# Eighteen loads of up to 62 KB a row in place of twenty-one of up to 54 KB, with V cut into units

## The chip, the cores and the metric

The kernel runs on one NeuronCore of one Trainium2 chip. Its five engines each follow their own instruction list: TensorE (PE in the profile), VectorE (DVE), ScalarE (ACT), GpSimd (POOL) and SyncE (SP), which here issues all transfers. Data comes from the chip's memory (HBM) over 16 DMA engines into the on-chip memory SBUF, which has 128 rows (partitions); matmul results go to PSUM banks. The metric is the device time of one execution in microseconds (us), as the median of several.

## The reference

One decode step (one new token, batch B = 2) of a block in which attention and a gated layer stand side by side:

```python
xn = layernorm(x)                       # x: (2, 1, 512)
q = (xn @ wq) -> 32 heads of 128
k, v = the last W = 2048 positions of k_cache, v_cache   # (2, 32, 2048, 128) each
p = softmax(q @ k.T * 128**-0.5)
att = (p @ v) -> (2, 1, 4096) @ wo
glu = ((xn @ w_gate) * (xn @ w_up)) @ w_down             # F = 1376
return x + att + glu
```

All is 32-bit floating point. K and V of one head are 2 MB each (2 x 2048 x 128 x 4 bytes), so 32 heads are 134 MB; with the weights 159.5 MB are read once, and little is computed on each number.

## The kernel before

**Layout.** The host writes all data in the order of use into one array, `stream`. A *load* is one transfer of that array: for each of the 128 rows of SBUF one contiguous piece of up to `STEP` = 54 KB. A *field* is a part of a load: K of head h (16 KB a row, written K5 below for head 5) with the part of `wq` that belongs to it (2 KB), V of head h (16 KB) with its rows of `wo` (2 KB), and the weights of the gated layer (`wg`, `wu`, `wd`, `wr`). `blocks` (line 54) returns the list of loads with their fields; host and kernel both use it. Behind a small load `f` come loads 0 to 20 (up to V of head 27), which are of 42 to 54 KB a row, and then the tail: load 21 (K31, V28), two of 18 KB (V29, V30), V31 with 16 KB, and three of 8, 4 and 2 KB. From K3 on, K and V alternate, V by LAG = 3 heads behind its K, three of the two kinds in each load: K V K in one, V K V in the next.

**Slots.** Three slots of 54 KB a row (`step0` to `step2`) take the loads in turn. `pump` (line 280) issues the next load when a slot has come free; `done` (line 301) counts the fields of a load that have been used, and calls `pump` at the last one. All loads go through SP's queue, in order. The instructions of all engines are written down in program order (`Flow.add`), and each waits for those earlier ones whose bytes it needs or overwrites. A load into a used slot therefore waits only for the instructions on the bytes that it overwrites. `x_nat` and `carry`, two transfers of a few KB, are issued behind the first three large loads.

**Work on a head.** For each K: DVE multiplies it by q (`products`, line 416) and sums over the 128 elements (`sums`), in place in the slot; maximum over a row and then over rows by POOL (`maxima`), exponentials by ACT (`weights`), whose result `p` stands in a ring of NP = 6 tiles, and the sum's reciprocal (`reciprocals`). PE projects q for a later group of four heads (`project_q`, line 399). For each V: `weigh` (line 468) multiplies it by p with 8 matmuls on PE, one for each 2 KB of the row (a *unit*); ACT copies the result (`copy_out`), PE transposes it with 4 matmuls (`transpose`), ACT scales it, and PE multiplies it by `wo` into the bank `acc` (`project_o`, line 504). `values` (line 518) does this for one head or for two at once, which share a bank, the copy and the transposes.

**Order.** The main loop (line 592) goes through the loads; behind the first K of a load stand all its V (`values(vs)`). PE works in program order, so a V matmul that waits for its load holds all that stands behind it. Heads 30 and 31 and the tail stand written out from line 617 on: `products(30)`, `sums(30)`, `values([26, 27])` of load 20, then V28, V29, V30, V31 each when its load has come, with some matmuls on other data (`keep_busy`) in between. DVE copies `acc` into SBUF (line 631) between products and sums of head 31.

The record of operations has one line, 226 (in `Flow.emit`), for all instructions; operations are told apart by their tiles: `step` is a slot, `q<-step,xnb` is `project_q`, `o_ps<-step,p` is `weigh`, `tr<-first,o_sb` is `transpose`, `acc<-step,oT` is `project_o`, `q<-xnb,mean_w` is `keep_busy`.

Of the kernel before, what the change touches and what calls it, by code (L numbers as in the profile page):

```python
# [14 lines left out]
P = 128  # L15
B, D, H, DH, SK, F = 2, 512, 32, 128, 8192, 1376
W = min(4096, max(256, SK // 4))
J = W // P
NC = D // P
FB = 4 * P  # L20
# [4 lines left out]
LAG = 3  # L25
# [6 lines left out]
GC = HG * DH  # L32
JG = J // 4
CK, CQ, CO = B * J * DH, NC * GC, D
CP = CQ // NC
UNIT = CK + max(CP, CO)
STEP = 3 * UNIT
WD = [(0, 2), (2, 4), (4, 7), (7, NFC - 1), (NFC - 1, NFC)]
NS = 3
BUFS = 3  # L40
# [13 lines left out]
def blocks():  # L54

    def wd(n):
        return [("wd", i, D) for i in range(*WD[n])]

    def k(h):
        return [("k", h, CK)] + ([("wq", h, CP)] if h + HG < H else [])

    def v(h):
        return [("v", h, CK), ("wo", h, CO)]  # L70

    def gu(half):
        n = NC * (FH[half][1] - FH[half][0])
        return [("wg", half, n), ("wu", half, n)]

    units = []
    for h in range(LAG, H - 1):
        units += [k(h), v(h - LAG)]
    ones = [("pick", 0, 8 * B), ("rows", 0, NFB * B)]
    first = [("x", 0, B * NC)] + ones + [("w", 0, NC * DH)]  # L80
    loads = [[("w", 1, CQ - NC * DH)] + k(0) + k(1), gu(0) + k(2)]
    loads += [gu(1) + units[0] + units[1] + wd(0) + [("wr", 0, NS * P)]]
    loads += [sum(units[i : i + 3], []) for i in range(2, len(units), 3)]
    loads += [k(H - 1) + v(H - 1 - LAG) + wd(1)]
    out = [(("f", 0), first)] + [(("s", i), fields) for i, fields in enumerate(loads)]
    late, last = ("s", len(loads)), ("s", len(loads) + 1)
    out += [(late, v(H - 3)), (late, v(H - 2)), (last, [("v", H - 1, CK)])]
    out += [(last, [("wo", H - 1, CO)] + wd(2))]
    return out + [(last, wd(n)) for n in range(3, len(WD))]


class Flow:
# [15 lines left out]
    def tile(self, shape, name, offset=None):  # L108
        if offset is None:
            size = -(-4 * math.prod(shape[1:]) // 32) * 32  # L110
            if self.low <= BASE < self.low + size:
                self.low = BASE + BUFS * 4 * STEP
            offset, self.low = self.low, self.low + size
# [141 lines left out]
def sliding_attention_plus_glu_kernel(  # L255
# [20 lines left out]
    tiles, used, left, got = {}, {}, {}, {}  # L276
# [54 lines left out]
        dve.memset(t, 0.0)  # L331
    gu_ps = o_ps

    NP = 6
    p_ring = [flow.tile([P, B, JG, 8 * B], f"p{i}") for i in range(NP)]
    for t in p_ring:
        pl.memset(t, 0.0)
# [40 lines left out]
    def side(h):  # L378

        return int(h % 3 == 0)  # L380
# [104 lines left out]
    def transpose(heads, o_sb):  # L485
        d = tr[:, 8 + 4 * bank : 12 + 4 * bank]
        s0, s1 = side(heads[0]), side(heads[-1]) + 1
        dst = d.rearrange("p (s b) -> p s b", b=B)[:, s0:s1, :]
        for r in range(4):
            pe.matmul(  # L490
                dst, o_sb[:, r * DH : (r + 1) * DH], pick[:, r, s0:s1, :],
                start=(r == 0), stop=(r == 3),
            )
        for h in heads:
            rec = rec_t.pop(h)
            oT[h] = oT_ring[h % 4]
            for b in range(B):
                c = B * side(h) + b
                act.activation(
                    oT[h][:, RB * b : RB * b + 1], d[:, c : c + 1], AF.Copy,  # L500
                    scale=rec[:, b : b + 1],
                )

    def project_o(h):
        wo = got["wo", h][0]
        if h < HF:
            pe.matmul(acc, oT.pop(h), wo, start=(h == 0), stop=False)
        else:
            accumulate(oT.pop(h), wo)
        done("wo", h)  # L510

    def pv(heads):
        for h in heads:
            weigh(h, got["v", h][0], range(CK // FB), h == heads[0], h == heads[-1])
            done("v", h)
        return copy_out()

    def values(heads, busy=((), ())):
        o_sb = pv(heads)
        for n in busy[0]:  # L520
            keep_busy(n)
        transpose(heads, o_sb)
        for n in busy[1]:
            keep_busy(n)
        for h in heads:
            project_o(h)


    hT = flow.tile([P, 4, NFB, M], "hT")
    dve.memset(hT, 0.0)  # L530
# [4 lines left out]
    def project_gu(half):  # L535
        lo, hi = FH[half]
        for w, kind in enumerate(("wg", "wu")):
            t = got[kind, half][0].rearrange("p (c f) -> p c f", c=NC)
            for c in range(NC):
                for n in range(2 * half, min(2 * half + 2, NFB)):  # L540
                    f0, f1 = n * FB, min(n * FB + FB, F)
                    pe.matmul(
                        gu_ps[w][32 * n : 32 * n + B, 0 : f1 - f0],
                        xn[:, c, :], t[:, c, f0 - lo : f1 - lo],
                        start=(c == 0), stop=(c == NC - 1),
                    )
            done(kind, half)
# [41 lines left out]
    spare_in = xnb.rearrange("p a b -> p (a b)")  # L589
    for i in range(2):  # L590
        project_first(i)
    for _, fields in blocks():
        ks = [i for kind, i, _ in fields if kind == "k"]
        vs = [i for kind, i, _ in fields if kind == "v"]
        if vs and vs[-1] >= H - 5:
            break
        for n, h in enumerate(ks):
            products(h)
            project_q(h)
            if 2 <= h <= 3:  # L600
                project_gu(h - 2)
            sums(h)
            if h == LAG:
                gate()
            if vs and n == 0:
                values(vs)
            if h == LAG:
                down(0)
                down_rest()
            maxima(h)  # L610
            weights(h)
            if h >= 1:
                reciprocals(h - 1)
# [3 lines left out]
    h = H - 2  # L617
# [1 line left out]
    spare, o_ps2 = spare_t[:, 0, :], spare_t[:, 1, :]  # L619
    products(h)  # L620
    sums(h)
    values([H - 6, H - 5], ((GC, 256), (GC,)))
    keep_busy(GC)
    maxima(h)
    reciprocals(h - 1)
# [1 line left out]
    o_sb = pv([HF])  # L627
# [7 lines left out]
    accumulate(carry, acc_sb)  # L635
    project_o(HF)
    weights(h)
    values([H - 3], ((GC,), (GC,)))
    maxima(h + 1)
    reciprocals(h)  # L640
    weights(h + 1)
# [2 lines left out]
    o_sb = pv([H - 2])  # L644
# [5 lines left out]
    o_sb = flow.ring([P, 4 * DH], "o_sb", 2)  # L650
    v = got["v", H - 1][0].rearrange("p (n k w) -> p n k w", k=2, w=2 * DH)
    for k, t in enumerate((o_ps[bank], o_ps2)):
        for n in range(CK // FB):
            b, i = divmod(n, JG)
# [19 lines left out]
def laid_out(x):  # L674

    import numpy as np

    a = x["A_x"].reshape(B, D)
    first = {
        kind: np.zeros((P, w), a.dtype) for kind, _, w in blocks()[0][1][:3]  # L680
    }
    carry = np.zeros((M, M), a.dtype)
    first["x"][:] = a.reshape(B, P, NC).transpose(1, 0, 2).reshape(P, B * NC)
    for b in range(B):
        for r in range(4):
            for s in range(2):
                first["pick"][8 * s + 4 * b + r :: 32, (2 * r + s) * B + b] = 1.0
        for n in range(NFB):
            first["rows"][32 * n + b, n * B + b] = 1.0
        carry[RB * b, RB * b] = 1.0  # L690
    cache = {
        kind: x[name][:, :, SK - W :, :].reshape(B, H, P, J * DH).transpose(1, 2, 0, 3)
        for kind, name in (("k", "A_k_cache"), ("v", "A_v_cache"))
    }
    wq = x["A_wq"].reshape(P, NC, H // HG, GC).transpose(2, 0, 1, 3)
    wo = x["A_wo"].reshape(H, P, D)
    gu = {
        kind: x[name].reshape(P, NC, F)
        for kind, name in (("wg", "B_w_gate"), ("wu", "B_w_up"))
    }  # L700
    wd = x["B_w_down"]
    rest = wd[NFC * P :].reshape(FR, NS + 1, P)

    def field(kind, i):
        if kind in first:
            return first[kind]
        if kind in ("k", "v"):
            return cache[kind][i].reshape(P, CK)
        if kind == "w":
            return (wq[0][:, :, DH:] if i else wq[0][:, :, :DH]).reshape(P, -1)  # L710
        if kind == "wq":
            return wq[i // HG + 1][:, i % HG, :]
        if kind == "wo":
            return wo[i]
        if kind == "wr":
            last = rest[:, NS, :].reshape(NS, FX, P).swapaxes(0, 1)
            return np.concatenate([rest[:, :NS, :], last]).reshape(P, NS * P)
        if kind == "wd":
            return wd[i * P : (i + 1) * P]
        return gu[kind][:, :, FH[i][0] : FH[i][1]].reshape(P, -1)  # L720

    def part(fields):
        rows = [field(kind, i) for kind, i, _ in fields]
        rows.append(np.zeros((P, pitch(fields) - sum(w for _, _, w in fields)), a.dtype))
        return np.concatenate(rows, axis=1).ravel()

    parts = [part(fields) for _, fields in blocks()]
    x_rows = np.zeros((D // P, 32 // RB, P), a.dtype)
    x_rows[:, :B] = a.reshape(B, D // P, P).transpose(1, 0, 2)
    return {  # L730
        "x_rows": x_rows.reshape(-1, P),
        "carry": carry,
        "stream": np.concatenate(parts),
    }
# [30 lines left out]
```

## Time and profile before

| | |
|---|---|
| median of 3 runs | 375.95 us (375.94 to 376.26) |
| the profiled execution | 376.07 us, its span 374.7 us |
| read from HBM | 159.47 MB |
| packets on the one DMA queue | 4370 |
| mean granted clock of TensorE | 0.80 of full speed |
| instructions | 2767 |

The span runs from the first to the last instruction; 1.4 us lie around it. A row of the timeline gives the start, the length, the engine, the operation with its output and inputs, how many records are merged in the row (`x16`), and in brackets how long the engine stood idle before it and what ended that. A matmul of 32-bit numbers leaves two records. In the rows of DMA issues the last number is the median time from issue to landing.

### The profile page before, as it was taken

How to read it: one execution, taken by the hardware profiler on the slowest of the kernel's cores; microseconds unless marked ns; L12 is line 12 of the kernel's file. 1: busy time of each engine (PE TensorE's matmuls, PEld its weight loads, DVE VectorE, ACT ScalarE, POOL GpSimd, SP SyncE). 2: the span in 40 equal slices, each digit the busy share in tenths (PEclk: the TensorE clock that was granted, in tenths of full speed). 3: DMA queues.
4: the chain of work that ended last, by engine and by line, in shares of the span. 5: the costliest groups of instructions: out<-in, count | busy, mean ns of one | idle time of the engine just before them, and what ended most of it. 6: DMA issues, size and time to landing. Idle time of an engine off the chain costs nothing.

```text
span 374.7 us, 2767 instructions
## 1 busy us (share of the span) xinstructions
PE 254.7 (68%) x1100; PEld 87.9 (23%) x1100; DVE 294.6 (79%) x147; ACT 58.7 (16%) x259; POOL 25.3 (7%) x78
## 2 busy tenths in 40 slices
PE   3386686986548486854848685485867548646997
PEld 3241122331112122211212221122212112121344
DVE  3299691998599499859949986994997699599960
ACT  1021001122020211202121120111202011121132
POOL 1001000000000000000000010000010000000010
PEclk9796988899696966859686688976668887656999
DMA  8999999899999999999999999999999999999996
GB/s 333 460 437 455 403 433 472 378 472 410 438 460 396 460 413 444 449 401 460 407 445 443 419 455 413 443 439 413 461 419 437 439 403 437 446 443 417 414 427 254
DMA packets 4382, 159.70 MB, mean 426 GB/s; under 512 B 514, under 2 KB 658, under 8 KB 1042
## 3 DMA queue, kind: packets, MB, share of 16 engines
q1 hardware_dynamic: 4370, 159.54, 98.7%
q8 instruction: 8, 0.13, 0.1%
q14 instruction: 4, 0.03, 0.0%
HBM read 159.47 MB, written 0.07 MB: 426 GB/s over the span
## 4 chain that ended last, share of the span: by engine, by line
DMA 69%; DVE 17%; PE 12%; ACT 1%; issue 1%; SPq 0%
DMA step<-in_stream_dram 69%; DVE step L226 8%; DVE s L226 8%; PE o_ps L226 4%; PE acc L226 4%; PE q L226 2%; PE tr L226 2%; ACT o_sb L226 0%; ACT oT L226 0%; SPq L226 0%; ACT hT L226 0%; DVE o_sb L226 0%; DVE m L226 0%; ACT hX L226 0%; DVE o_out L226 0%
## 5 line engine op out<-in xcount | busy, mean ns | idle before, releaser
L226 DVE TENSOR_TENSOR step<-step,q 128x4096 f32<-128x4096 f32 x31 | 136.7, 4408 | 53.2 <-DMA step<-in_stream_dram 53.2
L226 PE MATMUL q<-step,xnb 128*128 128x512 f32 (+1 forms) x128 | 92.3, 870 | 77.4 <-DMA step<-in_stream_dram 77.4
L226 DVE TENSOR_REDUCE s<-step 128x32 f32<-128x4096 f32 x32 | 141.4, 4419 | 1.1
L226 PE MATMUL o_ps<-step,p 128*16 128x512 f32 (+1 forms) x512 | 69.1, 677 | 10.5 <-DMA step<-in_stream_dram 10.4
L226 PEld LDWEIGHTS q<-step,xnb 128*128 128x128 f32 x128 | 32.0, 274 | 130.2 <-DMA step<-in_stream_dram 93.7
L226 PE MATMUL acc<-step,oT 128*9 128x512 f32 (+1 forms) x88 | 34.6, 548 | 9.0 <-ACT oT L226 9.0
L226 PE MATMUL tr<-first,o_sb 128*128 128x2 f32 (+2 forms) x198 | 27.7, 258 | 15.4 <-ACT o_sb L226 12.8
L226 ACT COPY o_sb<-o_ps 128x512 f32<-128x512 f32 (+1 forms) x24 | 13.9, 577 | 143.4 <-PE o_ps L226 143.4
L226 PEld LDWEIGHTS tr<-first,o_sb 128*128 128x128 f32 x198 | 25.6, 197 | 37.1 <-ACT o_sb L226 32.3
L226 POOL PARTITION_ALL_REDUCE mm<-m x32 | 11.3, 355 | 285.3 <-DVE m L226 274.8
L226 PEld LDWEIGHTS o_ps<-step,p 128*16 128x16 f32 x512 | 13.5, 106 | 70.6 <-issue 55.0
L226 ACT ACTIVATE nm<-mm 128x2 f32<-128x2 f32 x32 | 6.5, 203 | 129.2 <-POOL mm L226 129.2
L226 ACT ACTIVATE p<-s,nm 128x16 f32<-128x16 f32 x64 | 19.2, 300 | 1.0
L226 ACT ACTIVATE oT<-tr,rec 128x1 f32<-128x1 f32 x64 | 12.2, 260 | 28.3 <-PE tr L226 28.3
L226 POOL PARTITION_ALL_REDUCE sum<-rs x32 | 12.7, 398 | 52.5 <-ACT p L226 52.5
L226 PE MATMUL o_ps<-step,xn 128*2 128x512 f32 (+1 forms) x48 | 12.8, 586 | 0.0
L226 ACT ACTIVATION_READ_ACCUMULATOR p<-s,nm 128x1 f32 x64 | 11.9, 187 | 0.0
L226 DVE TENSOR_TENSOR step<-step,tr 128x4096 f32<-128x4096 f32 x1 | 4.4, 4420 | 9.5 <-DMA step<-in_stream_dram 9.5
L226 PEld LDWEIGHTS acc<-step,oT 128*9 128x9 f32 x88 | 4.2, 90 | 19.1 <-ACT oT L226 14.4
L226 PE MATMUL q<-xnb,mean_w 128*128 128x512 f32 (+1 forms) x18 | 8.5, 563 | 0.0
L226 PE MATMUL acc<-step,hT 128*9 128x128 f32 (+2 forms) x58 | 7.8, 356 | 0.0
L226 DVE TENSOR_TENSOR o_out<-acc,x_nat 128x128 f32<-128x128 f32 x1 | 0.3, 292 | 8.3 <-PE acc L226 8.3
(43 smaller groups left out, 42.2 us busy)
## 6 DMA issues: line engine op xcount, KB each, us to landing
step<-in_stream_dram SPq DMA_DIRECT2D x16, 6912.0 KB, 30.9
step<-in_stream_dram SPq DMA_DIRECT2D x2, 6400.0 KB, 33.0
step<-in_stream_dram SPq DMA_DIRECT2D x1, 6720.0 KB, 45.4
step<-in_stream_dram SPq DMA_DIRECT2D x1, 6656.0 KB, 29.2
step<-in_stream_dram SPq DMA_DIRECT2D x1, 5376.0 KB, 15.3
step<-in_stream_dram SPq DMA_DIRECT2D x1, 4864.0 KB, 31.7
step<-in_stream_dram SPq DMA_DIRECT2D x2, 2304.0 KB, 22.0
step<-in_stream_dram SPq DMA_DIRECT2D x1, 2048.0 KB, 23.6
```

Source lines behind the costliest of these rows:

```text
L226: made = getattr(eng, method)(*args, **kwargs)
```

## The change

`STEP` becomes 62 KB (31 units of 2 KB), with three slots as before. Up to V27 there are 18 loads, numbers 0 to 17, in place of 21. A table, `KS`, says how many K (with their `wq`) each begins with, one to three. What room is left is filled with units of V and with `wo`, in the order of the heads, so that a head's V may be cut at any of its 8 units and lie in two loads, and its `wo` may come a load later than its V. The first two loads have no V: K0 to K2 stand in load 0, all of `wg` and `wu` with K3 in load 1. The bytes and the tail's loads (K31 with V28, and so on) are as before.

`values` now goes through the fields of a load: it weighs the units that are there, and when a group's last unit has been weighed it copies, transposes and scales; a head is projected when it is scaled and its `wo` has come. The groups are as before heads 0; 1; 2 and 3; 4; 5 and 6; and so on up to 26 and 27. In the main loop `project_gu` of both halves stands in load 1. The tail is the same but for load 17: of its V, those units and `wo` that are not of heads 26 and 27 go ahead of these.

```diff
--- before.py
+++ after.py
@@ -34,7 +34,10 @@
 CK, CQ, CO = B * J * DH, NC * GC, D
 CP = CQ // NC
 UNIT = CK + max(CP, CO)
-STEP = 3 * UNIT
+STEP = 31 * FB
+NP = 6
+NV = CK // FB
+KS = [3, 1, 2, 1, 2, 2, 1, 2, 2, 2, 1, 2, 2, 2, 1, 2, 2, 1]
 WD = [(0, 2), (2, 4), (4, 7), (7, NFC - 1), (NFC - 1, NFC)]
 NS = 3
 BUFS = 3
@@ -73,14 +76,28 @@
         n = NC * (FH[half][1] - FH[half][0])
         return [("wg", half, n), ("wu", half, n)]
 
-    units = []
-    for h in range(LAG, H - 1):
-        units += [k(h), v(h - LAG)]
     ones = [("pick", 0, 8 * B), ("rows", 0, NFB * B)]
     first = [("x", 0, B * NC)] + ones + [("w", 0, NC * DH)]
-    loads = [[("w", 1, CQ - NC * DH)] + k(0) + k(1), gu(0) + k(2)]
-    loads += [gu(1) + units[0] + units[1] + wd(0) + [("wr", 0, NS * P)]]
-    loads += [sum(units[i : i + 3], []) for i in range(2, len(units), 3)]
+    ahead = [[("w", 1, CQ - NC * DH)], gu(0) + gu(1), [("wr", 0, NS * P)] + wd(0)]
+    pieces = [(h, n) for h in range(H - 1 - LAG) for n in range(NV + 1)]
+    loads, h = [], 0
+    for i, n in enumerate(KS):
+        fields = (ahead[i] if i < len(ahead) else []) + sum((k(h + j) for j in range(n)), [])
+        h += n
+        room = (STEP - sum(w for _, _, w in fields)) // FB if i > 1 else 0
+        taken, pieces = pieces[:room], pieces[room:]
+        for g in sorted({g for g, _ in taken}):
+            assert g < h - n
+            ns = [m for t, m in taken if t == g]
+            parts = [m for m in ns if m < NV]
+            if parts:
+                p0, p1 = parts[0], parts[-1] + 1
+                fields.append(("vp", (g, p0, p1), FB * (p1 - p0)))
+            if ns[-1] == NV:
+                fields.append(("wo", g, CO))
+        assert not pieces or pieces[0][0] >= h - NP
+        loads.append(fields)
+    assert not pieces and h == H - 1
     loads += [k(H - 1) + v(H - 1 - LAG) + wd(1)]
     out = [(("f", 0), first)] + [(("s", i), fields) for i, fields in enumerate(loads)]
     late, last = ("s", len(loads)), ("s", len(loads) + 1)
@@ -331,7 +348,6 @@
         dve.memset(t, 0.0)
     gu_ps = o_ps
 
-    NP = 6
     p_ring = [flow.tile([P, B, JG, 8 * B], f"p{i}") for i in range(NP)]
     for t in p_ring:
         pl.memset(t, 0.0)
@@ -515,16 +531,41 @@
             done("v", h)
         return copy_out()
 
-    def values(heads, busy=((), ())):
-        o_sb = pv(heads)
+    groups = [[0], [1]]
+    for h in range(2, H - 4, 3):
+        groups += [[h, h + 1], [h + 2]]
+    ready = []
+
+    def values(fields, busy=((), ())):
+        for kind, i, _ in fields:
+            if kind == "vp":
+                h, p0, p1 = i
+                heads = next(g for g in groups if h in g)
+                weigh(h, got[kind, i][0], range(p0, p1), h == heads[0], h == heads[-1])
+                done(kind, i)
+                if (h, p1) == (heads[-1], NV):
+                    o_sb = copy_out()
+                    for n in busy[0]:
+                        keep_busy(n)
+                    transpose(heads, o_sb)
+                    for n in busy[1]:
+                        keep_busy(n)
+                    ready.extend(heads)
+            elif kind == "wo":
+                arrived.append(i)
+            while ready and ready[0] in arrived:
+                project_o(ready.pop(0))
+
+    arrived = []
+
+    def value(h, busy):
+        o_sb = pv([h])
         for n in busy[0]:
             keep_busy(n)
-        transpose(heads, o_sb)
+        transpose([h], o_sb)
         for n in busy[1]:
             keep_busy(n)
-        for h in heads:
-            project_o(h)
-
+        project_o(h)
 
     hT = flow.tile([P, 4, NFB, M], "hT")
     dve.memset(hT, 0.0)
@@ -589,22 +630,23 @@
     spare_in = xnb.rearrange("p a b -> p (a b)")
     for i in range(2):
         project_first(i)
-    for _, fields in blocks():
+    for fields in [fields for key, fields in blocks() if key[0] == "s"]:
         ks = [i for kind, i, _ in fields if kind == "k"]
-        vs = [i for kind, i, _ in fields if kind == "v"]
-        if vs and vs[-1] >= H - 5:
+        kinds = [kind for kind, _, _ in fields]
+        if ks[0] == H - 2:
             break
         for n, h in enumerate(ks):
             products(h)
             project_q(h)
-            if 2 <= h <= 3:
-                project_gu(h - 2)
+            if n == 0 and "wg" in kinds:
+                project_gu(0)
+                project_gu(1)
             sums(h)
-            if h == LAG:
+            if n == 0 and "wg" in kinds:
                 gate()
-            if vs and n == 0:
-                values(vs)
-            if h == LAG:
+            if n == 0:
+                values(fields)
+            if n == 0 and "wr" in kinds:
                 down(0)
                 down_rest()
             maxima(h)
@@ -619,7 +661,9 @@
     spare, o_ps2 = spare_t[:, 0, :], spare_t[:, 1, :]
     products(h)
     sums(h)
-    values([H - 6, H - 5], ((GC, 256), (GC,)))
+    last_two = [f for f in fields if f[1] in (H - 6, H - 5) or f[0] == "vp" and f[1][0] >= H - 6]
+    values([f for f in fields if f not in last_two])
+    values(last_two, ((GC, 256), (GC,)))
     keep_busy(GC)
     maxima(h)
     reciprocals(h - 1)
@@ -635,7 +679,7 @@
     accumulate(carry, acc_sb)
     project_o(HF)
     weights(h)
-    values([H - 3], ((GC,), (GC,)))
+    value(H - 3, ((GC,), (GC,)))
     maxima(h + 1)
     reciprocals(h)
     weights(h + 1)
@@ -706,6 +750,9 @@
             return first[kind]
         if kind in ("k", "v"):
             return cache[kind][i].reshape(P, CK)
+        if kind == "vp":
+            h, p0, p1 = i
+            return cache["v"][h].reshape(P, CK)[:, FB * p0 : FB * p1]
         if kind == "w":
             return (wq[0][:, :, DH:] if i else wq[0][:, :, :DH]).reshape(P, -1)
         if kind == "wq":
```

How the change moves instructions is shown at two places. The first is PE's list around the last of the large loads. `p_58` to `p_60` are the weights of heads 25 to 27, `p_61` those of head 28; `step_49` to `step_51` are the three slots. Before, from the last load but one:

```order
L226 MATMUL o_ps<-step_50,p_58 16x512 x8
L226 MATMUL tr<-first,o_sb_117 128x2 x4
L226 MATMUL acc<-step_50,oT_64 9x512
L226 MATMUL o_ps<-step_51,p_59 16x512 x8
L226 MATMUL o_ps<-step_51,p_60 16x512 x8
L226 MATMUL q<-xnb,mean_w 128x512
L226 MATMUL q<-xnb,mean_w 128x256
L226 MATMUL tr<-first,o_sb_116 128x4 x4
```

And now:

```order
L243 MATMUL o_ps<-step_50,p_58 16x512 x5
L243 MATMUL o_ps<-step_51,p_58 16x512 x3
L243 MATMUL tr<-first,o_sb_117 128x2 x4
L243 MATMUL acc<-step_51,oT_64 9x512
L243 MATMUL o_ps<-step_51,p_59 16x512 x8
L243 MATMUL o_ps<-step_51,p_60 16x512 x8
L243 MATMUL q<-xnb,mean_w 128x512
L243 MATMUL q<-xnb,mean_w 128x256
L243 MATMUL tr<-first,o_sb_116 128x4 x4
```

Head 25 was weighed, transposed and projected from slot 50; now its last three units, and with them the transposes and the projection, read slot 51, the slot of heads 26 and 27, and stand ahead of these.

The second place is SP's list, the issues of the loads. Before, the first loads of `stream` up to the first that waits for a slot:

```order
L226 DMA step_49<-in_stream_dram 128x10752
L226 DMA step_50<-in_stream_dram 128x12800
L226 DMA step_51<-in_stream_dram 128x13440
L226 DMA x_nat<-in_x_rows_dram 16x128 [waits done_dve]
L226 DMA carry<-in_carry_dram 9x9
L226 DMA step_49<-in_stream_dram 128x13824 [waits done_pe,done_dve]
```

And now:

```order
L243 DMA step_49<-in_stream_dram 128x15360
L243 DMA step_50<-in_stream_dram 128x15616
L243 DMA step_51<-in_stream_dram 128x15744
L243 DMA x_nat<-in_x_rows_dram 16x128 [waits done_dve]
L243 DMA carry<-in_carry_dram 9x9
L243 DMA step_49<-in_stream_dram 128x15872 [waits done_pe,done_dve]
```

The three loads that are issued without a wait for a slot hold 46720 numbers a row where they held 36992, and the two small transfers still stand behind them.

## The prediction

> **What bounds the kernel now.** I read the page first, then the timelines of DVE and PE, then the chain of waits. The page says that the 16 DMA engines are never idle:
>
> ```profile
> PE 254.7 (68%) x1100; PEld 87.9 (23%) x1100; DVE 294.6 (79%) x147; ACT 58.7 (16%) x259; POOL 25.3 (7%) x78
> ...
> q1 hardware_dynamic: 4370, 159.54, 98.7%
> HBM read 159.47 MB, written 0.07 MB: 426 GB/s over the span
> DMA 69%; DVE 17%; PE 12%; ACT 1%; issue 1%; SPq 0%
> ```
>
> DMA queue 1 holds 98.7% of the span. How fast the stream runs between start and end is read where DVE waits for a load: it starts on a K the moment the load lands.
>
> ```profile
> 16.51 4.42 DVE L226 TENSOR_TENSOR step<-step,tr 128x4096 f32<-128x4096 f32 x1 [9.53 <-DMA step<-in_stream_dram]
> ...
> 47.51 4.42 DVE L226 TENSOR_TENSOR step<-step,q 128x4096 f32<-128x4096 f32 x1 [3.77 <-DMA step<-in_stream_dram]
> ...
> 65.31 4.42 DVE L226 TENSOR_TENSOR step<-step,q 128x4096 f32<-128x4096 f32 x1 [8.16 <-DMA step<-in_stream_dram]
> ...
> 97.89 4.42 DVE L226 TENSOR_TENSOR step<-step,q 128x4096 f32<-128x4096 f32 x1 [5.28 <-DMA step<-in_stream_dram]
> ...
> 106.98 4.40 DVE L226 TENSOR_TENSOR step<-step,q 128x4096 f32<-128x4096 f32 x1
> ...
> 293.49 4.42 DVE L226 TENSOR_TENSOR step<-step,q 128x4096 f32<-128x4096 f32 x1 [5.27 <-DMA step<-in_stream_dram]
> ```
>
> Between 97.89 (load 5) and 293.49 (load 17) twelve loads of 54 KB a row, 7.078 MB each, land in 195.60 us: 16.30 us a load, 434 GB/s, with no hole. Only load 3 comes late: 65.31 - 47.51 = 17.80 us, so 1.50 us are lost there. DVE needs 106.98 - 97.89 = 9.09 us for one K. The end is in the chain of waits:
>
> ```profile
> 340.62 0.04 issue
> 340.66 3.66 PE o_ps L226 x16
> 344.32 0.02 issue
> 344.34 23.63 DMA step<-in_stream_dram
> 367.97 0.04 issue
> 368.01 1.06 PE o_ps L226 x16
> ...
> 372.79 0.29 DVE o_out L226
> ```
>
> Load 20 (V26, K30, V27) lands at 340.62, V of head 31 at 367.97, and 6.7 us of PE, DVE and the write of the output follow. So the stream sets the time. But PE is right beside it over the last 34 us, which the chain hides and PE's timeline shows:
>
> ```profile
> 340.66 5.42 PE L226 MATMUL o_ps<-step,p 128*16 128x512 f32 x32 [7.12 <-DMA step<-in_stream_dram]
> 346.01 1.56 PE L226 MATMUL q<-xnb,mean_w 128*128 128x512 f32 x4
> ...
> 351.07 1.12 PE L226 MATMUL q<-xnb,mean_w 128*128 128x512 f32 x2
> 352.28 1.91 PE L226 MATMUL o_ps<-step,p 128*16 128x512 f32 x16
> ...
> 357.90 1.90 PE L226 MATMUL o_ps<-step,p 128*16 128x512 f32 x16
> ...
> 363.17 1.91 PE L226 MATMUL o_ps<-step,p 128*16 128x512 f32 x16 [0.23 <-DMA step<-in_stream_dram]
> ...
> 368.01 1.06 PE L226 MATMUL o_ps<-step,p 128*16 128x256 f32 x16 [0.17 <-DMA step<-in_stream_dram]
> ```
>
> From 340.66 to the end PE has no idle time but 0.09 us before V28 (351.07 + 1.12 = 352.19), 0.23 before V30 and 0.17 before V31: 0.49 us in all. The `q<-xnb,mean_w` rows are the fillers of `keep_busy`; they have a fixed length and PE's order is fixed, so nothing gives way if PE is late. **PE's slack in the tail is 0.49 us.**
>
> **The change, part by part.**
>
> *Fewer loads.* Up to V27 the bytes are the same (145.83 MB), in 18 loads instead of 21. What does a load cost beyond its bytes? Let R be the rate and c the price of one. The long stretch gives 16.30 = 7.078/R + c. From load 20's landing to V31's there are four loads and 11.796 MB in 367.97 - 340.62 = 27.35 us = 11.796/R + 4c. Together: c = 0.08 us, R = 436 GB/s. Bounds: nothing, and 0.5 us (the 1.50 us hole ahead of load 3, the largest, has three loads around it: the two small ones and load 3). I take 0.08, where the two equations meet: the last load with a K30 lands 3 x 0.08 = **0.24 us earlier**, at 340.38. The bounds are 0 and 1.5 us. Rows of 62 KB are not in the trace; 54 KB rows run at 434 GB/s and the tail's rows of 16 to 38 KB at 431, so I see no loss in longer ones. The hole itself I leave where it is, at no change: the two small loads still stand behind the third large one.
>
> The Trainium skill, "DMA: Bandwidth & Descriptors", section "Anatomy of one DMA — SWDGE (gpsimd) path", fits 2.0 us + bytes/436 GB/s to a DMA of the other issuing path. By it a load here would take 18.2 us and three fewer would save 6.0 us. The trace does not agree: 16.30 us a load, since the next one already stands in the queue.
>
> *Fewer, larger slots to wait for.* A load of 62 KB a row is 8.126 MB, 8.126/436 + 0.08 = 18.7 us. Now:
>
> ```profile
> step<-in_stream_dram SPq DMA_DIRECT2D x16, 6912.0 KB, 30.9
> ```
>
> So a load is issued 30.9 - 16.3 = 14.6 us before its own transfer begins. After the change the narrowest place is the start: load 0 has 18 KB a row more (2.36 MB, 5.4 us), lands at 21.9, and its three K take DVE until 21.9 + 27.3 = 49.2; then load 3 is issued. The queue runs empty with load 2, at 47.5 plus 4.98 MB more (11.4 us) = 58.9. Margin 9.7 us. K3 ends at 58.3, before load 2 lands, and from there two K (18.2 us) always fit into one load (18.7), so a slot comes free some 18 us before the queue runs dry. DVE's 5.4 us later start costs nothing: the stream covers it. If that cover went, each us of lateness would be one us of the end. PE is busy 68% of the span on average and its order within a load is the same kind; I take no stall. Sum: 0.
>
> *V in pieces.* The same 8 matmuls for a head, the same copies, transposes and projections, only cut differently between loads. Nothing is added in total; up to load 16 it lies in the shadow of the stream, with the margin above.
>
> *The last full load.* This is the place that costs. Load 20 held V26, K30 and V27; load 17 now holds K30, the last three units of V25, its wo, V26 and V27, and its last byte is the same byte of the stream. So at 340.38 PE has first to finish head 25: three units, the copy by ACT, four transposes, the scaling by ACT, one projection, all in order ahead of V26. Before, this was done 16 us earlier in a wait for DMA. The same steps of head 25 in the kernel before, there with eight units:
>
> ```profile
> 324.98 3.62 PE L226 MATMUL o_ps<-step,p 128*16 128x512 f32 x16 [2.90 <-DMA step<-in_stream_dram]
> 329.30 1.87 PE L226 MATMUL tr<-first,o_sb 128*128 128x2 f32 x8 [0.70 <-ACT o_sb L226]
> 331.67 1.88 PE L226 MATMUL acc<-step,oT 128*9 128x512 f32 x2 [0.50 <-ACT oT L226]
> ```
>
> One unit is two records of the `x` count. Narrower windows show what 8 of the first row's 16 records took, and 4 records at another place with the low clock:
>
> ```profile
> 324.98 1.91 PE L226 MATMUL o_ps<-step,p 128*16 128x512 f32 x8 [2.90 <-DMA step<-in_stream_dram]
> ```
> ```profile
> 199.45 1.06 PE L226 MATMUL o_ps<-step,p 128*16 128x512 f32 x4
> ```
>
> Each four records beyond the first four add 0.85 us, so they run in rounds of four. Six records lie between 1.06 and 1.91; I take 1.91, two rounds. Then 0.70 + 1.87 + 0.50 + 1.88: **6.86 us** at the low clock, on PE alone, with nothing beside it. Is the clock low there? It is where PE stood idle before, and it is lifted after a stretch of 3.4 us that is busy throughout:
>
> ```profile
> 327.20:330.60 3.40, 2.69 (x15) 1.30 (x7) 3.37 (x2) 0.59 (x1) 0.00 (x0) 0.50 0.90 392
> 330.60:334.00 3.40, 2.44 (x5) 0.58 (x5) 3.37 (x3) 0.41 (x2) 0.00 (x0) 0.50 0.90 392
> 340.90:344.30 3.40, 3.40 (x20) 0.68 (x16) 3.37 (x4) 0.67 (x4) 0.35 (x1) 0.50 0.93 401
> 344.30:347.70 3.40, 3.40 (x24) 1.37 (x16) 3.37 (x2) 0.81 (x3) 0.40 (x1) 1.00 1.14 485
> ```
>
> (The numbers are length, then busy PE, PEld, DVE, ACT, POOL, then the granted clock.) Busy 2.69 of 3.40 left it at 0.50; 3.40 of 3.40 raised it to 1.00. In the changed tail the 0.70 us gap falls into the first such stretch, so the lift comes one stretch later, by 347.7, just as V26 begins at 340.42 + 6.86 = 347.28. From there V26 and V27 run at the full clock, which costs less than before: 3.64 us of
>
> ```profile
> 313.53 3.64 PE L226 MATMUL o_ps<-step,p 128*16 128x512 f32 x32
> ```
>
> plus 0.2 for the half-clocked start, instead of 5.42. Late by 6.86 - 5.42 + 3.84 = **5.28 us**.
>
> *The sum.* V28 starts on PE at 352.19 - 0.24 + 5.28 = 357.23. By R and c its data lands at 340.38 + 11.5 = 351.9, V29's and V30's 5.5 us apart behind it (362.9), V31's at 367.8, so PE waits no more: 363.17 - 0.23 - 352.28 = 10.66 us to V30, 368.01 - 0.17 - 363.17 = 4.67 to V31, 374.70 - 368.01 = 6.69 to the end: 379.25, 4.55 us over the span of 374.70. Scores, maxima and weights of heads 30 and 31 shift with PE (DVE's copy of `acc` waits for it) and had their place before it. The profiled execution took 376.07, 0.12 over the median of 375.95; the sum is made against 376.07: **380.6 us**.
>
> Where the stretches of the clock lie decides a part of it. If the first stretch suffices in spite of the gap (2.7 of 3.4 is close), transposes and projection and the start of V26 take 1.4 us less: 379.2, and with a stretch that begins right with V25's units 1.6 us less: 379.0. If the lift comes 2 us later than I take it, 1 us more: 381.6. The Trainium skill, "TensorE: Matmul & The Clock Gate", Part 1, says that this window of 3.4 us runs free of the kernel's start. By that rule any of these places can turn up in a run, 379.0 to 381.6; the one execution here shows one place only.
>
> **Rivals.**
>
> *The stream pays more for a load than I take (not slower).* Place: between two loads of queue 1. If each of the three removed loads cost 1.6 us, load 17 would land 4.8 us earlier and the tail's loss (4.55 + 0.24) would be paid; from 1.35 us on the time is within 0.2%, and at 2.0 us (6.0 in all) it is 380.85 - 6.0 = 374.8. For it: the 1.50 us hole ahead of load 3 shows that a boundary can cost that. Against: twelve boundaries in a row cost 0.08 each. 4%.
>
> *The tail is hidden.* If PE did find the time for head 25, only the 0.24 us would be left: 375.8. For it: PE waits 7.12 us for DMA just ahead of 340.66. Against: the three units arrive with the same load, and 0.49 us is all the slack behind it. Even with the clock at 1.00 from the start, head 25 costs 0.9 + 0.7 + 1.05 + 0.5 + 1.05 = 4.2 us, and V26/V27 give 1.8 back: 377.7. 6% for the hidden tail.
>
> *A slot comes free too late.* Load 3 waits for three K where it waited for two. If the margin of 9.7 us were gone (PE holding load 1 or 0 longer), every load behind shifts: some 2 us more on top, 382.6. Against it: the issue 14.6 us ahead in the trace. 4%.
>
> **How the numbers follow.** Forecast (head 25 in PE's tail, 379.0 to 381.6): 86%; stream 4%, hidden 6%, slot 4%. About 0.2% (0.75 us) is what a measurement tells from no change. Faster by more needs the stream rival with its highest price: 3%. Within 0.2%: the hidden tail and the rest of the stream rival, 7%. Slower: 90%. The range reaches from 377.7 (the clock high from the start, which also covers a stream that gains 1.5 us) to 382.0 (late lift and a slightly late slot).
>
> **What would show it.** Right: load 17 lands near 340.4 and PE's timeline has there 3 units, a gap, transposes, a gap, one projection, then V26 near 347; V28 starts near 357 without a wait for DMA, and so do V30 and V31; the chain of waits runs on PE from load 17's landing to the end; queue 1's share falls, as the stream ends 4 to 5 us before the span does. Two loads of 62 KB land 37.4 us apart throughout. Wrong: DMA waits of PE before V30 and V31 (the tail was hidden), or a spacing of loads that differs from 18.7 us by more than 0.3, which would move the whole sum.

## The result and the profile after

The changed kernel takes 381.21 us (median of 4 runs, 381.04 to 381.63) against 376.11 for the kernel before (4 runs): 1.0137 times as long, with a 95% interval of 1.0124 to 1.0149. The forecast was 380.6. The profiled execution of the changed kernel took 381.04, its span is 379.7.

The page of the changed kernel, the rows that answer to those of before:

```profile
PE 261.7 (69%) x1100; PEld 90.7 (24%) x1100; DVE 295.2 (78%) x147; ACT 58.2 (15%) x259; POOL 25.3 (7%) x78
...
q1 hardware_dynamic: 3938, 159.54, 97.4%
HBM read 159.47 MB, written 0.07 MB: 420 GB/s over the span
...
DMA 63%; PE 21%; DVE 14%; ACT 2%; issue 0%; SPq 0%
```

The queue has 432 packets fewer (144 for each load that went), and its share of the span has fallen by 1.3 points: the stream ends where it ended before, and the span 5 us later. In the microsecond from 371.0 on, 127 GB/s were still moved before and 145 are now; in the next one 0 and 8. In the chain of waits PE's share went from 12% to 21%. The chain's last part, in order of time (start, length, what):

```profile
295.73 45.38 DMA step<-in_stream_dram
341.11 0.04 issue
341.16 1.94 PE o_ps L243 x6
343.10 0.02 issue
343.12 0.59 ACT o_sb L243
343.71 0.04 issue
343.76 1.88 PE tr L243 x8
345.64 0.02 issue
345.66 0.42 ACT oT L243 x2
346.09 0.04 issue
346.13 1.02 PE acc L243
...
377.79 0.29 DVE o_out L243
```

From load 17's landing at 341.11 to the end there is no DMA step any more. PE's timeline for the same stretch:

```profile
341.16 1.90 PE L243 MATMUL o_ps<-step,p 128*16 128x512 f32 x6 [4.95 <-DMA step<-in_stream_dram]
343.76 1.87 PE L243 MATMUL tr<-first,o_sb 128*128 128x2 f32 x8 [0.69 <-ACT o_sb L243]
346.13 1.02 PE L243 MATMUL acc<-step,oT 128*9 128x512 f32 x1 [0.50 <-ACT oT L243]
346.14 1.05 PE L243 MATMUL o_ps<-step,p 128*16 128x512 f32 x3
346.95 1.06 PE L243 MATMUL acc<-step,oT 128*9 128x512 f32 x1
346.97 5.11 PE L243 MATMUL o_ps<-step,p 128*16 128x512 f32 x29
352.01 1.56 PE L243 MATMUL q<-xnb,mean_w 128*128 128x512 f32 x4
...
358.12 1.91 PE L243 MATMUL o_ps<-step,p 128*16 128x512 f32 x16
...
368.60 1.90 PE L243 MATMUL o_ps<-step,p 128*16 128x512 f32 x16
...
373.07 1.05 PE L243 MATMUL o_ps<-step,p 128*16 128x256 f32 x16
```

Six records of head 25, a gap, its transposes, a gap, its projection, and heads 26 and 27. The first three records of V26 (346.14) stand beside the projection (346.13), not behind it. V28 starts at 358.12 where it started at 352.28, and none of V28, V30 (368.60) and V31 (373.07) has a wait for DMA in brackets. The clock in this stretch (windows; after PE, PEld, DVE, ACT and POOL stands the granted clock):

```profile
342.30:345.70 3.40, 2.63 (x11) 1.78 (x8) 3.37 (x2) 0.94 (x5) 0.40 (x1) 0.50 0.93 401
345.70:349.10 3.40, 2.97 (x16) 0.65 (x17) 3.40 (x1) 0.38 (x2) 0.00 (x0) 0.50 1.14 492
349.10:352.50 3.40, 3.40 (x23) 0.84 (x19) 1.21 (x3) 0.33 (x1) 0.35 (x1) 0.99 0.85 358
```

PE was busy 2.63 of 3.40 us with the 0.69 us gap in it, and the clock stayed at 0.50; after the next stretch, busy 2.97 of 3.40, it was at 1.00.

### The profile page after: what moved, and what is told of

The parts are those of the page before. It is cut to its first block, busy times and chain, and to the rows that moved or that the text cites. A ratio compares the mean times of both kernels' runs of the same rounds, so it can differ in the third digit from the quotient of the medians.

```text
span 379.7 us, 2753 instructions
## 1 busy us (share of the span) xinstructions
PE 261.7 (69%) x1100; PEld 90.7 (24%) x1100; DVE 295.2 (78%) x147; ACT 58.2 (15%) x259; POOL 25.3 (7%) x78
## 4 chain that ended last, share of the span: by engine, by line
DMA 63%; PE 21%; DVE 14%; ACT 2%; issue 0%; SPq 0%
DMA step<-in_stream_dram 63%; PE o_ps L243 7%; DVE s L243 7%; DVE step L243 7%; PE q L243 6%; PE acc L243 4%; PE tr L243 3%; ACT o_sb L243 1%; ACT oT L243 1%; DVE m L243 0%; SPq L243 0%; DVE o_out L243 0%; DVE rec L243 0%; SPq L242 0%
## 5 line engine op out<-in xcount | busy, mean ns | idle before, releaser
L243 PE MATMUL q<-step,xnb 128*128 128x512 f32 (+1 forms) x128 | 80.1, 773 | 72.6 <-DMA step<-in_stream_dram 72.6
L243 PE MATMUL o_ps<-step,p 128*16 128x512 f32 (+1 forms) x512 | 106.1, 764 | 10.2 <-DMA step<-in_stream_dram 10.2
L243 PEld LDWEIGHTS q<-step,xnb 128*128 128x128 f32 x128 | 28.7, 242 | 117.2 <-DMA step<-in_stream_dram 81.4
L243 PE MATMUL acc<-step,oT 128*9 128x512 f32 (+1 forms) x88 | 42.0, 638 | 9.1 <-ACT oT L243 9.1
L243 PE MATMUL tr<-first,o_sb 128*128 128x2 f32 (+2 forms) x198 | 29.8, 269 | 18.2 <-ACT o_sb L243 12.7
L243 PEld LDWEIGHTS o_ps<-step,p 128*16 128x16 f32 x512 | 18.8, 108 | 81.7 <-issue 69.2
L243 PEld LDWEIGHTS tr<-first,o_sb 128*128 128x128 f32 x198 | 27.6, 210 | 42.6 <-ACT o_sb L243 34.9
L243 ACT COPY o_sb<-o_ps 128x512 f32<-128x512 f32 (+1 forms) x24 | 13.8, 576 | 130.8 <-PE o_ps L243 130.8
L243 PE MATMUL o_ps<-step,xn 128*2 128x512 f32 (+1 forms) x48 | 10.5, 569 | 0.0
L243 DVE TENSOR_REDUCE m<-s 128x2 f32<-128x32 f32 x32 | 5.9, 186 | 1.1
L243 DVE RECIPROCAL rec<-sum 128x2 f32<-128x2 f32 x32 | 5.0, 155 | 2.2 <-POOL sum L243 2.2
```

The source lines that it names most:

```text
L243: made = getattr(eng, method)(*args, **kwargs)
```

## The experiments

The question was whether the place of head 25's last three units explains all of the 5.1 us, or whether the larger loads have a part in it.

**The tail alone, on the kernel before.** The 21 loads stay; only these units and their `wo` go from load 19 to the front of load 20.

```diff
-STEP = 3 * UNIT
+STEP = 31 * FB
...
+    rest = [("vp", (25, 5, 8), 3 * FB), ("wo", 25, CO)]
+    loads[19] = k(28) + [("vp", (25, 0, 5), 5 * FB)] + k(29)
+    loads[20] = rest + loads[20]
...
+    weigh(25, got["vp", i][0], range(5, 8), True, True)
+    done("vp", i)
+    o_sb = copy_out()
+    transpose([25], o_sb)
+    project_o(25)
     values([H - 6, H - 5], ((GC, 256), (GC,)))
```

> The kernel before, with its 21 loads, and only the last three units and the wo of head 25 moved from load 19 to the front of load 20 (42 and 60 KB; the slots are 62 KB for that). Theory: V28 starts 5.2 to 5.4 us later on PE, the 0.49 us of slack are used up, 380.3 to 381.8. Rival (the larger loads cost it): 376 as before.

Measured: 381.15 us, 1.0140 (1.0123 to 1.0157) times the kernel before. That is the whole loss, while no load is longer than before but load 20 itself (60 KB). PE in this run, at load 20:

```profile
340.59 1.90 PE L229 MATMUL o_ps<-step,p 128*16 128x512 f32 x6 [16.21 <-DMA step<-in_stream_dram]
343.19 1.87 PE L229 MATMUL tr<-first,o_sb 128*128 128x2 f32 x8 [0.69 <-ACT o_sb L229]
...
357.62 1.91 PE L229 MATMUL o_ps<-step,p 128*16 128x512 f32 x16
```

The same steps with the same lengths, and V28 17.0 us behind the first unit (357.62 - 340.59), as in the changed kernel (358.12 - 341.16).

**Load 17 in two transfers, on the changed kernel.** The 8 KB a row of head 25 come first, then the rest, into the same slot.

```diff
+        head = [f for f in fields if f[0] == "vp" and f[1][0] == 25 or f[:2] == ("wo", 25)]
+        if i == len(KS) - 1:
+            out += [(("s", i), head), (("s", i), [f for f in fields if f not in head])]
...
+        if not ks:
+            values(fields)
+            continue
         if ks[0] == H - 2:
             break
```

> The changed kernel with load 17 as two transfers into the same slot: first the three units and the wo of head 25 (8 KB a row), then K30, V26 and V27 (52 KB). All else, the 62 KB loads, the K ahead, the cut V, is as in the change. Theory (PE's tail): head 25's rest lands some 15 us before V26, PE does it while it waits, V26 starts right at the landing of the second part (near 341) and V28 near 352.5 as in the kernel before: 375.8 to 376.6. Rival (larger loads or the later start of K0 cost it): head 25's place does not matter, it stays at 380.5 to 381.5.

Measured: 380.98 us, 1.0125 (1.0107 to 1.0143). A miss for the theory as it stood: almost nothing came back, and the time is the rival's. But it does not show that the rival's reason is right: PE shows that the three units were done early, and what happened then:

```profile
329.59 2.29 PE L249 MATMUL o_ps<-step,p 128*16 128x512 f32 x13
342.73 1.87 PE L249 MATMUL tr<-first,o_sb 128*128 128x2 f32 x8 [10.85 <-ACT o_sb L249]
```

The matmuls end at 331.9, but the transposes wait 10.85 us for ACT's copy, and V26, which lands meanwhile, waits behind them on PE. ACT's timeline says why:

```profile
341.28 0.20 ACT L249 ACTIVATE nm<-mm 128x2 f32<-128x2 f32 x1 [8.14 <-POOL mm L249]
341.52 0.31 ACT L249 ACTIVATE p<-s,nm 128x16 f32<-128x16 f32 x1
...
342.12 0.56 ACT L249 COPY o_sb<-o_ps 128x512 f32<-128x512 f32 x1
```

In program order the copy stands behind the weights of head 29, whose maximum comes from DVE only at 341. The matmuls had left the tail; the copy, the transposes and the projection had not. In the changed kernel the same weights end at 342.6, half a microsecond before the copy is due (343.12), so this second wait was hidden behind the first and took its place.

**The same, with head 25 ahead of head 29's weights in program order.**

```diff
         if not ks:
-            values(fields)
             continue
...
+            if h == H - 3:
+                values(next(f for key, f in blocks() if key == ("s", len(KS) - 1)))
             maxima(h)
             weights(h)
```

> As the run with load 17 in two transfers, and in program order the work on head 25 stands before the maxima and weights of head 29, so that ACT's copy of head 25 no longer stands behind the weights of head 29, which wait for DVE until 342.2. Theory (it takes both, the landing and ACT's queue, to free PE's tail): head 25 is finished near 332, V26 starts at the landing of the second part, 375.8 to 376.7. Rival (the 62 KB loads cost it in a way not yet seen): 380 to 381.5.

Measured: 376.13 us, 0.9999 (0.9990 to 1.0008) of the kernel before, over 11 runs. PE:

```profile
336.50 1.05 PE L249 MATMUL tr<-first,o_sb 128*128 128x2 f32 x8 [0.72 <-ACT o_sb L249]
338.06 1.43 PE L249 MATMUL acc<-step,oT 128*9 128x512 f32 x2 [0.50 <-ACT oT L249]
340.70 5.92 PE L249 MATMUL o_ps<-step,p 128*16 128x512 f32 x32 [1.21 <-DMA step<-in_stream_dram]
```

Head 25 is finished at 339.5, V26 starts when it lands, and the loss is gone with all the large loads in place. On this way it takes both, the landing and ACT's queue. The moment was missed: head 25 was expected to be finished near 332. Its matmuls ended at 331.9 in the run before, but here they ran at a granted clock of 0.50 until 335.1 and ended at 335.8; the margin before V26 lands, 1.2 us, is smaller than was reckoned. What is left of the change, 62 KB loads and two fewer of them, has no effect that 11 runs can tell from none: V31, too, starts on PE when it lands, at 367.97, where it started at 368.01 before.

**The order on PE alone.** Load 17 stays whole; the units of head 25 and all of heads 26 and 27 are weighed first, and head 25's transposes and projection stand where fillers were.

```diff
-    last_two = [f for f in fields if f[1] in (H - 6, H - 5) or f[0] == "vp" and f[1][0] >= H - 6]
-    values([f for f in fields if f not in last_two])
-    values(last_two, ((GC, 256), (GC,)))
+    o_sbs = []
+    for g in ([25], [26, 27]):
+        for kind, i, _ in [f for f in fields if f[0] == "vp" and f[1][0] in g]:
+            weigh(i[0], got[kind, i][0], range(i[1], i[2]), i[0] in (25, 26), i[0] == g[-1])
+            done(kind, i)
+        o_sbs.append(copy_out())
+    transpose([25], o_sbs[0])
+    keep_busy(256)
+    project_o(25)
+    transpose([26, 27], o_sbs[1])
     keep_busy(GC)
+    project_o(26)
+    project_o(27)
```

> The changed kernel with another order on PE in load 17 alone: the three units of head 25, then the 16 of heads 26 and 27, and only then the transposes and the projection of head 25, where fillers stood (two of the four fillers of this place are left out). Theory (a chain of head 25 with two waits for ACT at the low clock, ahead of V26): about 6.4 us of matmuls without a gap, 0.75 us more than in the kernel before until V28, 376.0 to 377.5. Rival (the amount of work behind load 17 sets it, whatever the order): 379.5 to 381.

Measured: 376.40 us, 1.0008 (0.9999 to 1.0018). PE:

```profile
340.92 6.54 PE L243 MATMUL o_ps<-step,p 128*16 128x512 f32 x38 [5.14 <-DMA step<-in_stream_dram]
347.39 1.05 PE L243 MATMUL tr<-first,o_sb 128*128 128x2 f32 x8
```

The 38 records run without a gap in 6.54 us (expected 6.4). V28 starts at 352.73, 11.81 us behind the first unit; it was 11.62 in the kernel before and 16.96 in the changed kernel. But two fillers of 512 columns are left out as well, and in the changed kernel such a filler holds the next row by 1.03 to 1.05 us (354.22 to 355.25, 357.07 to 358.12). By this estimate about 2.1 of the 5.2 us that V28 gained are the missing fillers and about 3.1 the order; no run leaves these fillers out in the old order.

**The clock.** Fillers on PE just ahead of load 17, four in one run and seven in another.

```diff
     spare, o_ps2 = spare_t[:, 0, :], spare_t[:, 1, :]
+    for _ in range(7):
+        keep_busy(GC)
     products(h)
```

> The changed kernel with four fillers (512 columns each) on PE ahead of what waits for load 17, so that PE's clock is at 1.00 when it lands. Theory: head 25 costs 4.2 us in place of 6.9, V26 and V27 3.6 in place of 5.0, V28 starts some 14 us after load 17's landing in place of 17.0: 377.8 to 378.8. Rival (the gaps for ACT set it, not the clock): 380.5 to 381.3. If a filler runs into the landing, up to 1 us more in both.

> The changed kernel with seven fillers of 0.93 us ahead of what waits for load 17; four ended 3.3 us before the landing in the profiled execution and the clock fell back to 0.50. Theory (clock): now it is at 1.00 at the landing in every execution, V28 starts some 14 us after it, 377.9 to 378.9 with little spread. Rival (gaps for ACT alone): 380.5 to 381.3.

Measured: with four 379.35 us (378.85 to 381.11), with seven 378.16 us (377.86 to 380.07), that is 1.0095 (1.0071 to 1.0119) and 1.0065 (1.0044 to 1.0085) times the kernel before. With four the time lies between the ranges of the theory and of the rival. With seven it lies in that of the theory, but the spread is not little: one of the four executions took 380.07. The profiled execution with four was its slowest, 381.11, and its row shows why: the fillers ended early and the clock was back at 0.50 when load 17 came.

```profile
333.62 3.70 PE L243 MATMUL q<-xnb,mean_w 128*128 128x512 f32 x8
340.64 1.90 PE L243 MATMUL o_ps<-step,p 128*16 128x512 f32 x6 [3.32 <-DMA step<-in_stream_dram]
```

With seven they reach up to the landing:

```profile
335.27 6.28 PE L243 MATMUL q<-xnb,mean_w 128*128 128x512 f32 x14
341.48 1.04 PE L243 MATMUL o_ps<-step,p 128*16 128x512 f32 x6
343.22 1.05 PE L243 MATMUL tr<-first,o_sb 128*128 128x2 f32 x8 [0.70 <-ACT o_sb L243]
...
355.28 1.91 PE L243 MATMUL o_ps<-step,p 128*16 128x512 f32 x16
```

V28 starts 355.28 - 341.48 = 13.8 us behind the first unit, 17.0 in the changed kernel (358.12 - 341.16). In the kernel before it was 11.62, at 0.50 when V26 landed. So of the 5.3 us that head 25 adds here, 3.2 are gone at the full clock, and 2.2 remain: the two gaps for ACT and the matmuls themselves. The last filler ends at 341.55 (335.27 + 6.28), so the fillers, and not the landing, set the start of the first unit in this execution.

**The hole at the start.** The two small transfers are taken out of the queue and come as fields of the first load; once on the kernel before, once on the kernel with load 17 split and head 25 early.

```diff
-    first = [("x", 0, B * NC)] + ones + [("w", 0, NC * DH)]
+    first = [("x", 0, B * NC)] + ones + [("xn", 0, P), ("cy", 0, 16), ("w", 0, NC * DH)]
...
-    sp.dma_start(x_nat[::RB, :], x_rows)
+    x_nat = got["xn", 0][0]
...
-    sp.dma_start(carry, carry_rows)
+    carry = got["cy", 0][0][:M, :M]
```

> The kernel before with its 21 loads, only the two small transfers gone, as fields of the first load. Theory (the hole of 1.50 us ahead of load 3 is theirs): load 3 lands near 64, 374.5 to 375.2. Rival: 376.0 to 376.3.

> As the run before it, and the two small transfers are gone: x_nat and carry come as fields of the first load (70 KB more there, 0.16 us). Theory (the hole of about 1.4 us around load 2 belongs to the two small transfers behind it): the whole stream comes 1.2 to 1.4 us earlier, 374.4 to 375.4. Rival (the hole has another cause): 375.9 to 376.9.

Measured: 376.35 us, 1.0005 (0.9997 to 1.0014), and 376.08, 0.9999 (0.9990 to 1.0008). A miss in both. In the first, load 2 still lands at 47.67 and load 3 17.28 us behind it:

```profile
47.67 4.42 DVE L226 TENSOR_TENSOR step<-step,q 128x4096 f32<-128x4096 f32 x1 [3.77 <-DMA step<-in_stream_dram]
...
64.95 4.42 DVE L226 TENSOR_TENSOR step<-step,q 128x4096 f32<-128x4096 f32 x1 [7.30 <-DMA step<-in_stream_dram]
```

That is 0.52 us less than the 17.80 of the kernel before, so 0.98 of the 1.50 us of the hole are still there. And the 0.36 us by which load 3 came earlier (64.95 for 65.31) were gone at load 9, which landed at 163.21, where it was 163.09 before. In the second, load 2 lands at 60.45, where it was 60.20 with the two transfers (0.16 us were expected for the larger first load). So the small transfers are not the cause of most of the hole, and the kernel is no faster without them; what the cause is, stays open.

## Why the prediction was right

*PE's slack in the tail is 0.49 us.* Right in kind, and it decided the case: the tail on the kernel before and the split load with head 25 early show it from both sides. In size it was some 0.4 us more. V28 starts 5.84 us later than before (358.12 for 352.28) and V31 5.06 (373.07 for 368.01), so 0.78 us were taken up between the two, not the 0.40 of the two brackets. A row's length reaches beyond the start of the next row: before, V30 started 0.63 us behind the start of the projection ahead of it (363.17 - 362.54), now 0.22 (368.60 - 368.38), so the bracket of 0.23 stands for a wait of 0.41; for V31 the 0.17 stand for 0.35 (368.01 - 367.43 = 0.58, now 0.23).

*Head 25 ahead of V26, late by 5.28 us.* Right in kind: the steps up to the projection took 1.90 + 0.69 + 1.87 + 0.50 (1.91, 0.70, 1.87 and 0.50 were taken), and that the lift of the clock needs a second stretch was right. V28 stood 17.01 us behind the landing where the sum had 357.23 - 340.38 = 16.85. That this is so near is luck, for two errors of some 2 us cancel. The projection did not hold V26: it began 5.03 us behind the landing (346.14 - 341.11), where the sum had 6.90 (347.28 - 340.38). And from there to V28 it took 11.98 us (358.12 - 346.14), where the sum had 9.95: the lift came at 349.1, not at 347.7, so that V26 and V27 ran for 3 us at 0.50, where the sum had 0.4, and the projection shared these first rounds with V26. From V28 on PE took 368.60 - 358.12 = 10.48 to V30 (10.66) and 4.47 to V31 (4.67), by the waits that the brackets had shown too short.

*Load 17 lands 0.24 us earlier, at 340.38.* Wrong by 0.73: it landed at 341.11, 0.49 later than load 20 before. Most loads did land 18.7 us apart, as worked out, but two did not. DVE's waits in the changed kernel:

```profile
60.30 4.42 DVE L243 TENSOR_TENSOR step<-step,q 128x4096 f32<-128x4096 f32 x1 [1.27 <-DMA step<-in_stream_dram]
...
79.03 4.42 DVE L243 TENSOR_TENSOR step<-step,q 128x4096 f32<-128x4096 f32 x1 [0.49 <-DMA step<-in_stream_dram]
...
98.07 4.42 DVE L243 TENSOR_TENSOR step<-step,q 128x4096 f32<-128x4096 f32 x1 [9.87 <-DMA step<-in_stream_dram]
...
266.38 4.42 DVE L243 TENSOR_TENSOR step<-step,q 128x4096 f32<-128x4096 f32 x1 [0.46 <-DMA step<-in_stream_dram]
...
285.10 4.42 DVE L243 TENSOR_TENSOR step<-step,q 128x4096 f32<-128x4096 f32 x1 [0.48 <-DMA step<-in_stream_dram]
...
304.35 4.42 DVE L243 TENSOR_TENSOR step<-step,q 128x4096 f32<-128x4096 f32 x1 [10.08 <-DMA step<-in_stream_dram]
```

From 98.07 (load 4) to 266.38 (load 13) nine loads take 18.70 us each, but load 4 came 19.04 behind load 3 and load 15 19.25 behind load 14, 0.9 us more together than two of the others. This lies outside the bounds of this term, which were 0 to 1.5 us of gain, and a spacing that differs from 18.7 us by more than 0.3 was one of the signs that I had named for being wrong. In the other runs with these loads, load 4 comes 18.70 to 19.21 behind load 3 and load 15 18.69 to 18.92 behind load 14, and single others are late (load 7, 19.03 us, with four fillers; load 10, 19.02, with head 25 early); the cause is open. The 0.08 us that I put on a load were not seen; the kernel with load 17 split and head 25 early has two loads fewer and its ratio is 0.9999 (0.9990 to 1.0008).

*The hole ahead of load 3 stays where it is.* The amount was right, the place was not. Load 2 landed at 60.30, 1.4 us later than the 58.9 worked out, and load 3 18.73 behind it, without a hole. The reason that I gave, the two small transfers, did not hold in the two runs without them.

*The slots.* Right, no load came late for want of a slot: load 3 was issued at

```profile
49.23 0.35 SPq L243 DMA_DIRECT2D step<-in_stream_dram  x1
```

(49.2 was worked out), 11 us before load 2 landed, and the others up to load 17 at least 9.7 us before the one ahead of them had landed (load 8 at 144.43, load 7 landed at 154.17). The 18 us that I gave for the later ones do not hold for all.

*The sum.* 379.25 was the span, 379.7 came; the landing gave +0.73, the tail up to V28 +0.16, the rest -0.44 (two shorter pieces and the end). That it came so close rests on terms of 0.2 to 0.7 us that partly cancel, and within the tail on the two of 2 us named above.

*The rivals.* The stream that pays for a load was refused by the kernel with load 17 split and head 25 early. The hidden tail gave 375.8 by the sum, and where an experiment did hide it, 376.13 was measured. The price of the tail at the full clock was put at 377.7; with seven fillers 378.16 were measured, in an execution whose first unit started 1.06 us later than the sum had it (341.48 for 340.42), behind the last filler.

What the prediction had not seen is the second wait: ACT's weights of head 29 end at 342.6 in the changed kernel. The run with load 17 in two transfers brought the units early, and the time stayed at 380.98; nothing in the sum tells why.

## What to carry to other kernels

Here a stream of transfers set the time and the next one always stood in the queue, and larger transfers then gained nothing that could be measured. What counted was what the engines still had to do behind each landing near the end, and a filled-up load can put work there that used to be done in a wait. Read the slack of the last engine in its timeline, not in the chain of waits, which shows only the transfer. And when such work is moved forward, follow it through every in-order engine that it passes: here the data, then ACT's queue held it, and moving the data gave the time back only together with the order on ACT. Another order on PE alone, with two fillers fewer, gave it back as well.

## What the runs showed of the hardware that was not expected

In the changed kernel TensorE's clock fell at 338.9 and rose at 349.2, three stretches of 3.4 us apart. Of these the last, from 345.75 to 349.17, was busy for 3.04 us (89%), and 1.00 followed it; the one ahead of it, with the gap of 0.69 us in it, was busy for 2.59 us (76%) and was followed by 0.50. How near the limit lies shows the kernel with load 17 in two transfers, where the clock fell at 336.65 and rose at 350.25, four such stretches apart. Its stretch with a gap of 0.50 us was busy for 2.92 of 3.42 us (85%), and the clock stayed at 0.50 for a further stretch:

```profile
343.44:346.86 3.42, 2.92 (x18) 1.47 (x22) 3.39 (x2) 0.41 (x2) 0.00 (x0) 0.50 0.89 387
```

The ends of matmuls are modelled, so these shares are not exact. The Trainium skill, "TensorE: Matmul & The Clock Gate", Part 1, speaks of a busy window of about 3.4 us; the rows here say how busy it was.

A hole of 1.0 to 1.5 us stands in the stream early on in every kernel here: ahead of load 3 with loads of 42 to 54 KB (17.28 to 17.80 us for a load that takes 16.30), and up to load 2 with 60 to 62 KB (it landed at 60.05 to 60.47, where 58.9 was worked out), with and without the two small transfers. No run here shows its cause.
